# Turning gathered rows by DMA transposes of 16-bit halves, with y kept as planes of halves

## Chip, core and metric

The kernel runs on one core of one Trainium2 chip. The metric is the device time of one execution in microseconds (us). A core has five engines that work side by side, each through its own queue in order: TensorE (PE; its weight loads are shown as PEld), VectorE (DVE), ScalarE (ACT), GpSimd (POOL) and SyncE (SP), which here only issues DMAs. Sixteen DMA engines move data for the queues of SP and POOL.

## What is computed

First a filter along the sequence, through a real Fourier transform, for 8 sequences of 2496 rows with 256 channels. Then a mixture of experts on its 19,968 rows: each row goes to the two of 8 experts that score highest.

```python
y = irfft(rfft(x, axis=1) * (filt_r + 1j * filt_i), n=2496, axis=1)
x = y.reshape(19968, 256)
noisy = x @ w_gate + log1p(exp(x @ w_noise)) * noise
top2 = argpartition(-noisy, 2, axis=1)[:, :2]      # weights: softmax over the two
for e in range(8):
    for k in range(2):
        mask = top2[:, k] == e
        h = maximum(x[mask] @ w1[e], 0)            # w1: 256 x 1024
        out[mask] += top2_w[mask, k, None] * (h @ w2[e])   # w2: 1024 x 256
```

All of it is fp32. Products are made by splitting an operand into a rounded high part and the rest (`_split`, the pairs named h and l) and adding three matmuls (`_mm3`).

## The kernel before

**Stages.** `fft_stream` makes the filtered rows, one sequence ("batch", `bt`) after another, in halves of 128 channels (`n = 2 * bt + h`). The last step of a half, `i2` (L505), copies 117 x 512 values from PSUM into `yt` (L523) and stores them to `y` in DRAM (L527). A row of `y` has 256 channels and 8 gate weights, `YW` = 264 words. `gate` and `route` score the rows and write, for each expert, lists of row numbers (`lst`). The expert stage starts when the first batch is routed and runs beside the stream for the later batches; at the end it is alone.

**Blocks.** `expert` (L1068) works through blocks of 512 listed rows (`nt` = 4 tiles of 128) of one expert; two blocks in a row share an expert's weights from the third batch on (`PAIRS`). What is left is done in blocks of 256 (`UNIT`, `nt` = 2). For each block:

- `gather` (L986): POOL fetches rows of `y` by indirect DMA, 128 to a tile, into slots `xg` of the SBUF tile `stage` (L992). There are 8 slots, two blocks.
- `turn` (L999): the rows lie with rows on partitions, and the matmuls need channels on partitions. TensorE transposes each tile, for the channel halves `kc` = 0 and 1, into the PSUM bank `xps` (L1008); ACT rounds the high part into `mxh` (L1012) and DVE subtracts for `mxl` (L1013). POOL copies the expert's gate weights into `gt` (L1017).
- First layer (L1086 to L1100): for each of 8 slices f of the hidden width, six matmuls into a PSUM bank (`hps`, or for f = 2 and 5 one of the two `yps` banks, L1088), then ACT makes `hh` (L1095) and DVE `hl` (L1096).
- Second layer (L1109 to L1135): for each tile t, 16 or 24 matmuls into `yps` (L1120, L1121 or `_mm3`), scaled by the gate weight on ACT (L1125) and DVE (L1127) into a slot `yo`, and added to `out` by an indirect DMA of POOL (L1128).

`front` (L967) begins a block with new weights: `load_w` has SP load w1 and w2 through four slots `wst` (L1029), and `wsplit` splits them on ACT and DVE (L1057, L1058).

**What sets the order.** The kernel is written as Python generators, and a scheduler then orders the instructions of each engine by a timeline of its own, with data dependencies and buffer reuse kept. `pin` keeps some instructions in written order: those of the stream's opening, and POOL's gathers. In `expert` the next block's gather is written at the head of a block (`fetch`, L1061, at most two blocks ahead), and its `turn` between the two layers of the block before (L1104 to L1106). So the next block's rows are turned while the second layer runs. Each of `mxh0`, `mxl0`, `mxh1`, `mxl1` has one buffer, which the first layer of the block before must have read. Once built, every queue is in order: an instruction that waits holds all behind it on its engine, and SP's and POOL's DMA issues are such instructions.

## Time and profile before

| | us |
|---|---|
| three timed runs | 2311.85, 2312.91, 2316.61 (median 2312.91) |
| profiled execution, first to last instruction | 2318.9 |
| POOL: gathers (L992), busy | 328.8 (320 of 1.027) |
| POOL: scatters (L1128), busy | 526.9 (320 of 1.647) |
| ACT: `mxh` (L1012), busy | 96.8 (178 of 0.544) |
| DVE: `mxl` (L1013), busy | 113.1 (178 of 0.635) |
| HBM read, written | 221.98 MB, 105.78 MB |

The profile is of one execution and gives no other time for it than its span. Busy time of an engine is the time in which any of its instructions ran; matmuls are pipelined, so the start of one falls before the end of the one ahead, and the distance from start to start is what one costs the stream. The `idle before` of a group is the time its engine stood still just ahead of it, with what ended that. The profile's chain that ended last holds only the final scatter, so it says nothing on the middle of the run; slices and stretches do.

### The profile page before, as it was taken

The page shows a single profiled execution, that of the slowest core. Times are in us where ns is not written, and L with a number is a line of the kernel's source. Part 1 is how long each engine was busy: PE and PEld are TensorE (multiplying, and loading weights), DVE is VectorE, ACT ScalarE, POOL GpSimd, SP SyncE. Part 2 cuts the span into 40 slices and gives each one's busy share as a digit, 9 for nine tenths or more (in the row PEclk, how much of TensorE's full clock was granted, in tenths as well). Part 3 has the DMA queues.
Part 4 walks back from the last instruction along what each step waited for, and adds up shares of the span by engine and source line. Part 5 has one row for each costly group of instructions (what it writes and reads, how often), then busy time and mean ns, then how long its engine had stood idle before and what let it go on. Part 6 is the DMA issues. An engine that isn't in the chain of part 4 may idle for free. (4 is left out here: it accounts for less than half of the span.)

```text
span 2318.9 us, 39299 instructions
## 1 busy us (share of the span) xinstructions
PE 2263.9 (98%) x13089; PEld 1899.9 (82%) x13089; DVE 1544.4 (67%) x3331; ACT 1189.3 (51%) x2373; POOL 927.8 (40%) x827
## 2 busy tenths in 40 slices
PE   8889999999999999999999999999999999999998
PEld 6448888888788888888888888888888888889997
DVE  4866797778668665875669666954444445557886
ACT  6655646654554554444544444444444444446775
POOL 4014244332334334443434433544544454535442
PEclk9989999999999999999999999999999999999999
DMA  8677757665654555464454553444444445567773
GB/s 238 201 240 181 199 136 199 180 157 121 168 138 117 147 136 128 115 149 115 111 131 96 129 141 84 95 94 98 92 91 88 97 92 129 122 183 226 217 217 87
DMA packets 284723, 329.64 MB, mean 142 GB/s; under 512 B 37371, under 2 KB 197603, under 8 KB 284515
## 3 DMA queue, kind: packets, MB, share of 16 engines
q1 hardware_dynamic: 222435, 241.61, 34.4%
q0 software_dynamic: 62080, 85.47, 21.7%
q8 instruction: 105, 1.72, 0.3%
q14 instruction: 103, 0.84, 0.1%
HBM read 221.98 MB, written 105.78 MB: 141 GB/s over the span
## 5 line engine op out<-in xcount | busy, mean ns | idle before, releaser
L1120 PE MATMUL yps<-w,hh 128*128 128x512 f32 x2112 | 747.1, 398 | 0.0
L1128 POOL DMA_INDIRECT out<-stage,ids x320 | 526.9, 1647 | 330.5 <-DVE stage L1127 131.6
L1121 PE MATMUL yps<-w,hl 128*128 128x256 f32 x2112 | 570.9, 280 | 0.6 <-DVE hl L1096 0.6
L992 POOL DMA_INDIRECT stage<-y,ids x320 | 328.8, 1027 | 581.8 <-PE xps L1008 198.7
L121 PE MATMUL hps<-mxl,w1h 128*128 128x512 f32 (+1 forms) x1424 | 535.1, 376 | 0.0
L120 PE MATMUL hps<-mxh,w1h 128*128 128x512 f32 (+1 forms) x1424 | 526.5, 380 | 3.5 <-DVE hl L1096 1.5
L122 PE MATMUL hps<-mxh,w1l 128*128 128x512 f32 (+1 forms) x1424 | 527.1, 371 | 0.0
L1096 DVE SCALAR_TENSOR_TENSOR hl<-hps,hh 128x512 fp32r<-128x512 f32 (+1 forms) x712 | 438.5, 631 | 122.2 <-ACT hh L1095 117.7
L1095 ACT ACTIVATE hh<-hps 128x512 fp32r<-128x512 f32 (+1 forms) x712 | 381.2, 555 | 223.8 <-PE hps L122 204.3
L1120 PEld LDWEIGHTS yps<-w,hh 128*128 128x128 f32 x2112 | 389.2, 188 | 80.4 <-ACT hh L1095 0.3
L1121 PEld LDWEIGHTS yps<-w,hl 128*128 128x128 f32 x2112 | 396.9, 188 | 19.6 <-DVE hl L1096 1.0
L120 PEld LDWEIGHTS hps<-mxh,w1h 128*128 128x128 f32 x1424 | 265.7, 189 | 51.8 <-issue 4.1
L122 PEld LDWEIGHTS hps<-mxh,w1l 128*128 128x128 f32 x1424 | 269.0, 189 | 45.8
L121 PEld LDWEIGHTS hps<-mxl,w1h 128*128 128x128 f32 x1424 | 269.1, 189 | 40.6 <-issue 0.2
L1125 ACT ACTIVATE stage<-yps,gt 128x256 f32<-128x256 f32 x320 | 143.3, 474 | 284.6 <-PE yps L1121 140.0
L1127 DVE SCALAR_TENSOR_TENSOR stage<-yps,gt,stage 128x256 f32<-128x256 f32 x264 | 120.9, 479 | 196.5 <-ACT stage L1125 133.0
L1013 DVE TENSOR_TENSOR mxl<-xps,mxh 128x512 fp32r<-128x512 f32 (+1 forms) x178 | 113.1, 635 | 152.4 <-ACT mxh L1012 148.7
L1012 ACT CAST mxh<-xps 128x512 fp32r<-128x512 f32 (+1 forms) x178 | 96.8, 544 | 221.5 <-PE xps L1008 188.8
L1058 DVE TENSOR_TENSOR w<-stage,w 128x512 fp32r<-128x512 f32 x216 | 143.6, 685 | 29.3 <-ACT w L1057 23.9
L964 POOL CAST ids<-lt 128x8 int32<-128x8 f32 (+2 forms) x63 | 14.6, 231 | 369.4 <-DMA lt<-lst 330.4
L1058 DVE TENSOR_TENSOR w1l<-stage,w1h 128x512 fp32r<-128x512 f32 x180 | 123.7, 687 | 55.7 <-ACT w1h L1057 37.6
L1057 ACT CAST w1h<-stage 128x512 fp32r<-128x512 f32 x180 | 111.8, 621 | 95.5 <-PE hps L121 47.8
(222 smaller groups left out, 3073.8 us busy)
## 6 DMA issues: line engine op xcount, KB each, us to landing
stage<-w SPq DMA_DIRECT2D x396, 256.0 KB
x<-x SPq DMA_DIRECT2D x88, 256.0 KB
fd<-c SPq DMA_DIRECT2D x77, 240.0 KB
wb<-w SPq DMA_DIRECT2D x18, 1024.0 KB
fx<-fd SPq DMA_DIRECT2D x140, 128.0 KB
out<-z SPq DMA_DIRECT2D x24, 702.0 KB
y<-yt SPq DMA_DIRECT2D x40, 248.6 KB
y<-yt SPq DMA_DIRECT2D x40, 234.0 KB
```

The lines of the kernel that those rows point to most:

```text
L120: nc.tensor.matmul(o, lh, rh, start=start, stop=False)
L121: nc.tensor.matmul(o, lh, rl, start=False, stop=False)
L122: nc.tensor.matmul(o, ll, rh, start=False, stop=stop)
L992: self.pin(lambda: self.nc.gpsimd.indirect_dma_start(out=x, out_offset=None, in_=self.y[:BLK + ready * ROWS], in_offset=bass.IndirectOffse ...
L1058: nc.vector.tensor_sub(l, sv, f32v(h))
L1095: nc.scalar.activation(h, p, AF.Relu)
L1096: nc.vector.scalar_tensor_tensor(l, p, 0.0, f32v(h), op0=ALU.max, op1=ALU.subtract)
L1120: nc.tensor.matmul(bank, h, hl, start=(f == 0), stop=False)
L1121: nc.tensor.matmul(p, l, hl[:, 0], start=False, stop=(f == 7))
L1125: nc.scalar.activation(o, p, AF.Copy, scale=gate[:, t])
L1127: nc.vector.scalar_tensor_tensor(o, bank[:, 1], gate[:, t], o, op0=ALU.mult, op1=ALU.add)
L1128: a = nc.gpsimd.indirect_dma_start(out=self.io["out"][:BLK + ready * ROWS], out_offset=bass.IndirectOffsetOnAxis(ap=ids[:, t:t + 1], axis= ...
```

## The change

`y` now keeps each 128-channel half of a row as two planes of 16-bit halves: `i2` writes from PSUM, read as 16-bit, first the 128 low halves and then the 128 high halves. The bytes of a row are as many as before, and the gate weights stay as they were. The tensors are declared as 32-bit integers for the DMAs, which only carry them.

TensorE's transposes go. A new function `flip` has SP issue one DMA transpose of 16-bit elements for each gathered tile, 128 rows x 512 halves, into `xt`, [128, 4, 512] 16-bit with one buffer: channel on the partition, and for each `kc` a plane of low and a plane of high halves. POOL's copy of the gate weights moves into `flip`, and the register with the expert's number is loaded in `gather`. `turn` then has DVE put the halves together, a 16-bit copy from two planes into interleaved pairs in a slot `x32` of `stage` (one slot, used for both `kc`), and ACT and DVE split from there as before. `flip` is called after a gather is issued and at the end of each `turn`, and does nothing while a turned block has not been used.

To make room, `xg` has 4 slots instead of 8, `yo` 5 instead of 6, `stage` is 5120 words wide, and two tiles of the gate (`uh`, `oh0`) share buffers with `ut0` and `gl`. In the first layer f = 2 and f = 5 take the freed `xps` bank instead of `yps`.

```diff
-        self.y = self.dp.tile([NROW, YW], F32, name="y")
+        self.y = self.dp.tile([NROW, YW], I32, name="y")
...
-        at, n, w = {"wst": (0, 4, 512), "xg": (2048, 8, YW), "yo": (2048 + 8 * YW, 6, 256)}[nm]
+        at, n, w = {"wst": (0, 4, 512), "xg": (2048, 4, YW), "yo": (2048 + 4 * YW, 5, 256), "x32": (2048 + 4 * YW + 5 * 256, 1, 512)}[nm]
...
-            self.uh = P.tile([120, 24, 16], R32, name="uh")
+            self.uh = P.tile([120, 24, 16], R32, name="uh", tag="ut0", bufs=1)
...
-        nc.scalar.copy(yt[:, :k, :128], p[:RP, :m].rearrange("p (g d) -> p g d", g=k))
+        nc.scalar.copy(yt.bitcast(U16)[:, :k, :256].rearrange("p g (two d) -> p g two d", two=2),
+                       p.bitcast(U16)[:RP, :2 * m].rearrange("p (g d two) -> p g two d", g=k, two=2))
...
+    def flip(self):
+        e = next((e for e in self.ahead if not e[3]), None)
+        if e is None or self.turned is not None:
+            return
+        e[3] = True
+        nc, nt = self.nc, e[0][2]
+        xg, at, ra = e[2]
+        xt = self.P.tile([128, 4, 512], U16, name="xt", bufs=1)[:, :, :128 * nt]
+        for t in range(nt):
+            nc.sync.dma_start_transpose(xt[:, :, 128 * t:128 * t + 128], xg[t].bitcast(U16)[:, :2 * D])
+        gate = self.P.tile([128, 4, 1], F32, name="gt", bufs=3)[:, :nt]
...
+        nc.gpsimd.tensor_copy(gate, rows[:, :, bass.ds(ra, 1)])
+        self.turned = xt, gate
...
-            q = self.PS.tile([128, 512], F32, name="xps", bufs=1)
-            for t in range(nt):
-                nc.tensor.transpose(q[:, t * 128:(t + 1) * 128], xg[t][:, kc * 128:(kc + 1) * 128], self.ident)
+            q = self.slot("x32")
+            nc.vector.tensor_copy(q.bitcast(U16)[:, :2 * w].rearrange("p (t two) -> p two t", two=2), xt[:, 2 * kc:2 * kc + 2])
...
+        self.turned = None
         xT.append(gate)
+        self.flip()
         return xT
...
-                self.ahead.append((*p, self.gather(*p)))
+                self.ahead.append([*p, self.gather(*p), False])
+                self.flip()
...
-                p = self.PS.tile([128, 512], F32, name="hps", tag="hps" if f % 3 < 2 else "yps", bufs=2)[:, :w]
+                p = self.PS.tile([128, 512], F32, name="hps", tag="hps" if f % 3 < 2 else "xps", bufs=2 if f % 3 < 2 else 1)[:, :w]
```

What the scheduler makes of it shows at three places late in the run, where blocks of 512 rows come in pairs. On TensorE, before, where one block's second layer (`yps`) ends and the next one's first layer (`hps`) begins; the numbers in names tell tiles apart:

```order
L1121 MATMUL yps_20729<-w2_20452,hl_20633 128x256
L120 MATMUL hps_20806<-mxh0_20694,w1h_20669 128x512
L1008 MATMUL xps_20698<-ident_70,stage_83 128x128 x4
L121 MATMUL hps_20806<-mxl0_20695,w1h_20669 128x512
L122 MATMUL hps_20806<-mxh0_20694,w1l_20670 128x512
L1120 MATMUL yps_20709<-w2_20452,hh_20643 128x512
```

The same place now, where L1140 and L1141 are the old L1120 and L1121, and L121 to L123 the old L120 to L122:

```order
L1141 MATMUL yps_19892<-w2_19852,hl_19838 128x256
L121 MATMUL hps_19956<-mxh0_19856,w1h_19612 128x512
L121 MATMUL hps_19978<-mxh0_19856,w1h_19616 128x512
L1140 MATMUL yps_19872<-w2_19852,hh_19848 128x512
L1140 MATMUL yps_19892<-w2_19852,hh_19848 128x512
L122 MATMUL hps_19956<-mxl0_19857,w1h_19612 128x512
```

The four transposes are gone from between the first layer's matmuls, which still begin after two of the four second-layer groups. On SP, before, between the loads of w2 (L1029) and the register loads for the next list (`tabi`):

```order
L1029 ISA
L1029 DMA stage_83<-w2 128x512
L958 ISA
L958 DMA lt_17112<-lst_61 128x2x4
L973 TENSOR_LOAD tabi_15579
L973 ISA x2
L956 TENSOR_LOAD tabi_15579
```

And now (L1048 is the old L1029, L963 the old L958):

```order
L1048 ISA
L1048 DMA stage_83<-w2 128x512
L963 ISA
L963 DMA lt_16984<-lst_61 128x2x4
L1014 DMA_TRANSPOSE xt_16852<-stage_83 128x4x128 x4
L978 TENSOR_LOAD tabi_15478
L978 ISA x2
L961 TENSOR_LOAD tabi_15478
```

A block's four transposes stand in SP's queue behind the loads of w2 and the list. On DVE, before, from the split of a turned block (`mxl`) over the second layer's evictions (`yps`) to the next first layer's (`hl`):

```order
L1013 TENSOR_TENSOR mxl1_19104<-xps_19098,mxh1_19103 128x512
L1127 SCALAR_TENSOR_TENSOR stage_83<-yps_19109,gt_18903,stage_83 128x256
L1127 SCALAR_TENSOR_TENSOR stage_83<-yps_19129,gt_18903,stage_83 128x256
L1058 TENSOR_TENSOR w1l_19304<-stage_83,w1h_19303 128x512
L1127 SCALAR_TENSOR_TENSOR stage_83<-yps_19149,gt_18903,stage_83 128x256
L1096 SCALAR_TENSOR_TENSOR hl_19201<-hps_19193,hh_19200 128x512
```

And now (L1028 is the new copy, L1033, L1077, L1116 and L1147 the old L1013, L1058, L1096 and L1127):

```order
L1028 COPY stage_83<-xt_19184 128x2x512
L1033 TENSOR_TENSOR mxl1_19417<-stage_83,mxh1_19416 128x512
L1147 SCALAR_TENSOR_TENSOR stage_83<-yps_19427,gt_18967,stage_83 128x256
L1147 SCALAR_TENSOR_TENSOR stage_83<-yps_19447,gt_18967,stage_83 128x256
L1077 TENSOR_TENSOR w1l_19613<-stage_83,w1h_19612 128x512
L1028 COPY stage_83<-xt_19420 128x2x512
L1147 SCALAR_TENSOR_TENSOR stage_83<-yps_19467,gt_18967,stage_83 128x256
L1116 SCALAR_TENSOR_TENSOR hl_19519<-hps_19511,hh_19518 128x512
```

The copy that empties `xt_19184` lets SP transpose the following block into `xt_19420`, and only five rows later stands the copy that needs it, ahead of the third `yps` eviction and of the next block's `hl`.

More of the change, by code (lines that the diff above doesn't have):

```diff
@@ L965, in read_list, with front @@
         return ids, n, nt, s, self.tabs[i]
-    def front(self, blk, xg, fill=None):
+    def front(self, blk, fill=None):
         nc = self.nc
@@ L979, in front @@
             fill()
-        if fill and self.held_any:
-            xT = self.pin(self.turn, xg, nt, hold=False, only=[self.nc.tensor.engine])
-        else:
-            xT = self.turn(xg, nt)
+        xT = self.turn(nt)
         return w1, xT, w2st
@@ L996, in gather, with turn @@
             xg.append(x)
-        return xg, self.turns["xg"] + 1 - nt
-    def turn(self, xg, nt):
+        return xg, self.turns["xg"] + 1 - nt, self.ra
+    def flip(self):
[9 more added lines that the diff above has]
+        gate = self.P.tile([128, 4, 1], F32, name="gt", bufs=3)[:, :nt]
+        rows = self.stage[:, 2048:2048 + 4 * YW].rearrange("p (s w) -> p s w", w=YW)[:, at:at + nt, D:]
+        nc.gpsimd.tensor_copy(gate, rows[:, :, bass.ds(ra, 1)])
+        self.turned = xt, gate
+    def turn(self, nt):
         nc, P = self.nc, self.P
         xT = []
-        xg, at = xg
+        xt, gate = self.turned
         w = 128 * nt
         for kc in range(2):
-            q = self.PS.tile([128, 512], F32, name="xps", bufs=1)
-            for t in range(nt):
-                nc.tensor.transpose(q[:, t * 128:(t + 1) * 128], xg[t][:, kc * 128:(kc + 1) * 128], self.ident)
+            q = self.slot("x32")
+            nc.vector.tensor_copy(q.bitcast(U16)[:, :2 * w].rearrange("p (t two) -> p two t", two=2), xt[:, 2 * kc:2 * kc + 2])
             h = P.tile([128, 512], R32, name=f"mxh{kc}", bufs=1)
@@ L1014, in turn @@
             xT.append((h, l))
-        gate = P.tile([128, 4, 1], F32, name="gt", bufs=3)[:, :nt]
-        rows = self.stage[:, 2048:2048 + 8 * YW].rearrange("p (s w) -> p s w", w=YW)[:, at:at + nt, D:]
-        nc.gpsimd.tensor_copy(gate, rows[:, :, bass.ds(self.ra, 1)])
+        self.turned = None
         xT.append(gate)
+        self.flip()
         return xT
@@ L1078, in expert @@
             if cur is None:
-                cur = self.front(blk, xg, fill)
+                cur = self.front(blk, fill)
             w1, xT, w2st = cur
@@ L1104, in expert @@
             if self.ahead:
-                b2, i2, x2 = self.ahead[0]
-                cur = (w1, self.turn(x2, nt), None) if i2 else self.front(b2, x2, fill if late else None)
+                b2, i2 = self.ahead[0][:2]
+                cur = (w1, self.turn(nt), None) if i2 else self.front(b2, fill if late else None)
             self.fetch(may)
```

19 lines of the change are left out of this document (11 added, 8 removed).

## The prediction

> **What bounds the kernel now.** I read the page first: its head, the busy times, the forty slices.
>
> ```profile
> span 2318.9 us, 39299 instructions
> PE 2263.9 (98%) x13089; PEld 1899.9 (82%) x13089; DVE 1544.4 (67%) x3331; ACT 1189.3 (51%) x2373; POOL 927.8 (40%) x827
> PE   8889999999999999999999999999999999999998
> PEclk9989999999999999999999999999999999999999
> DMA  8677757665654555464454553444444445567773
> ```
>
> TensorE is idle for 2318.9 - 2263.9 = 55 us in all, and from the fourth slice on it is never under nine tenths, at the full granted clock. So the kernel is bound by TensorE's own work, not by a wait. Three stretches of 58 us (busy time of PE, PEld, DVE, ACT, POOL in turn; then clock, DMA share, GB/s) say how far the next engine is behind: a stretch with routing, one with experts alone, one with 256-row blocks.
>
> ```profile
> 1218.00:1276.00 58.00, 58.00 (x326) 48.33 (x325) 53.91 (x146) 26.51 (x52) 25.36 (x21) 1.00 0.44 98
> 1740.00:1798.00 58.00, 58.00 (x304) 49.01 (x303) 27.61 (x46) 24.62 (x47) 29.07 (x27) 1.00 0.42 90
> 2146.00:2204.00 58.00, 58.00 (x411) 54.01 (x410) 47.91 (x98) 41.47 (x98) 26.41 (x29) 1.00 0.74 219
> ```
>
> VectorE has 30 us to spare where experts run alone, but only 4 us where rows are routed and 10 us in the 256-row blocks.
>
> **What goes from TensorE.** The groups by line and shape give the transposes, and the stream of instructions shows what they hold up (start, duration; x4 is four in a row):
>
> ```profile
> L1008 PE MATMUL xps<-ident,stage 128*128 128x128 f32 x640 | 102.9, 274 | 12.3 <-DMA stage<-y,ids 5.4 <-issue 4.1 <-DVE mxl L1013 1.4
> 1502.58 0.60 PE L1008 MATMUL xps<-ident,stage 128*128 128x128 f32 x4
> 1502.93 0.47 PE L121 MATMUL hps<-mxl,w1h 128*128 128x512 f32 x1
> 1503.25 0.40 PE L122 MATMUL hps<-mxh,w1l 128*128 128x512 f32 x1
> 1503.48 0.40 PE L517 MATMUL q<-th,hl 120*117 120x512 f32 x1
> 2150.65 0.39 PE L1120 MATMUL yps<-w,hh 128*128 128x512 f32 x1
> 2150.88 0.27 PE L1121 MATMUL yps<-w,hl 128*128 128x256 f32 x1
> 2151.00 0.63 PE L1120 MATMUL yps<-w,hh 128*128 128x512 f32 x2
> ...
> 2151.82 0.38 PE L1008 MATMUL xps<-ident,stage 128*128 128x128 f32 x2
> 2151.95 0.36 PE L121 MATMUL hps<-mxl,w1h 128*128 128x256 f32 x1
> 2152.15 0.29 PE L122 MATMUL hps<-mxh,w1l 128*128 128x256 f32 x1
> 2152.28 0.62 PE L1120 MATMUL yps<-w,hh 128*128 128x512 f32 x2
> ```
>
> Busy times of pipelined matmuls overlap, so I don't take the 102.9 us; I take start to start. Four transposes hold the stream for 1502.93 - 1502.58 = 0.35 us, and the matmul behind them takes 0.32 us to the next start where its neighbour takes 0.23: 0.09 more. Together 0.44 us. Two transposes: 0.13 us, and 0.20 against 0.13 behind them: 0.20 us. A turn has two groups (kc = 0 and 1). Each turn makes two evictions on ACT and two on DVE, whose rows (quoted below) count 142 of 512 columns and 36 of 256, so 71 blocks of 512 rows and 18 of 256, 89 turns. Saved: 142 x 0.44 + 36 x 0.20 = 62.5 + 7.2 = **70 us**. Bounds: 142 x 0.35 + 36 x 0.13 = 54 us if the matmul behind keeps its delay, 102.9 us if the row's busy time were all exclusive.
>
> **What VectorE and ScalarE get.** DVE puts the halves together, 178 copies (142 of 1024 16-bit elements, 36 of 512), a kind that the trace lacks. The nearest rows:
>
> ```profile
> L1013 DVE TENSOR_TENSOR mxl<-xps,mxh 128x512 fp32r<-128x512 f32 x142 | 97.8, 689 | 143.7 <-ACT mxh L1012 141.8 <-issue 1.2
> L1013 DVE TENSOR_TENSOR mxl<-xps,mxh 128x256 fp32r<-128x256 f32 x36 | 15.3, 424 | 8.6 <-ACT mxh L1012 6.8
> L734 DVE TENSOR_SCALAR gz<-rank 117x176 f32<-117x176 f32 x8 | 2.0, 252 | 0.3
> L771 DVE TENSOR_TENSOR rank<-rank 117x176 f32<-117x176 f32 x40 | 13.6, 339 | 0.5
> L523 ACT COPY yt<-q 117x512 f32<-117x512 f32 x80 | 46.9, 586 | 35.2 <-PE q L517 21.4 <-PE q L516 5.1 <-PE q L513 4.7
> L523 ACT COPY yt<-q 117x256 f32<-117x256 f32 x16 | 6.1, 379 | 1.4 <-DMA y<-yt 0.6 <-ACT stage L1125 0.5 <-PE q L513 0.2
> L1095 ACT ACTIVATE hh<-hps 128x512 fp32r<-128x512 f32 x568 | 329.5, 598 | 204.1 <-PE hps L122 184.6 <-PE yps L122 4.9 <-issue 4.6
> L1096 DVE SCALAR_TENSOR_TENSOR hl<-hps,hh 128x512 fp32r<-128x512 f32 x568 | 381.5, 685 | 110.3 <-ACT hh L1095 105.8 <-issue 1.9 <-PE yps L122 0.7
> ```
>
> Two-source work costs (689 - 424) / 256 = 1.035 ns an element; at that rate a copy of 1024 takes 689 + 512 x 1.035 = 1.22 us. But a one-source operation in SBUF is cheaper: 252 against 339 ns at 176 elements, 87 ns less, half of 176 x 1.035. The copy is one-source in SBUF, so I take half rate: 0.69 us (0.42 for the small one). Added: 142 x 0.69 + 36 x 0.42 = 113 us (1.22 and 0.69: 198 us); DVE goes from 67% to some 74%. In the routing stretch about 2.2 turns bring 2.2 x 2 x 0.69 = 3.0 us into 4.1 us of room, and 5.4 us at the high price: 0 to 1.3 us over, in eight such stretches 0 to 10 us. The 256-row stretch takes 4.5 x 2 x 0.42 = 3.8 us into 10. I take 3 us. ACT's `yt` copy now names 1024 elements where it named 512: (586 - 379) / 256 = 0.81 ns each, so 80 x 0.41 + 16 x 0.21 = 36 us, hidden on an engine that is 51% busy; without that cover it would cost those 36 us. The banks: f = 2 and f = 5 now share one `xps` bank instead of two `yps` banks. Two groups of six matmuls at 0.23 us, 2.8 us, stand between them, and the eviction that must be through takes 0.60 on ACT and 0.69 on DVE, 1.28 us; so nothing, and if that cover is gone, the excess of a late eviction once in a block. In return the second layer no longer shares its `yps` banks. The turn's chain (copy, ACT, DVE, twice, through one `x32` buffer) is 2 x (0.69 + 0.60 + 0.69) = 4.0 us, 0.7 longer than with two groups of transposes. Beside it lie the two second-layer groups that TensorE's order puts before the next block's first matmuls, 16 pairs at 2151.00 - 2150.65 = 0.35 us, 5.6 us. Five `yo` slots for six and the gate's shared buffers I cost at nothing: TensorE, idle for 55 us in all, is not waiting for them today. If that cover is gone too, they belong to the late rows below.
>
> **What the DMA engines and SP get.** 320 transposes of 128 x 512 halves, 128 KB each. The trace has none; the nearest are the queues and SP's issues:
>
> ```profile
> q1 hardware_dynamic: 222435, 241.61, 34.4%
> q0 software_dynamic: 62080, 85.47, 21.7%
> L1029 SPq DMA_DIRECT2D stage<-w x360: 3/333/1957, 120.7 to 2062.0; - x180
> SPq L1029 <- DVE w1l L1058: 405.1, 119, 15.1
> L1128 POOL DMA_INDIRECT out<-stage,ids x320 | 526.9, 1647 | 330.5 <-DVE stage L1127 131.6 <-ACT stage L1125 111.5 <-issue 54.6
> ```
>
> SP's queue moves 241.61 MB in 34.4% of the span, 798 us: 0.43 us for 128 KB. POOL's moves rows of a kilobyte at 85.47 MB in 503 us: 0.77 us. Over 320 transposes that is 138 to 246 us on top of 34.4 + 21.7 = 56.1%, 1301 us: 62 to 67%, room enough. At the far end a transpose may go packet by packet, a 256-byte row of 128 halves each: 512 packets at POOL's 503 x 16 / 62080 = 0.130 us on one of 16 engines make 4.2 us, 320 of them 1331 us. I take 0.43 us, nearest in queue. An issue on SP costs between 0.33 us (median of L1029) and the 1.65 us that POOL spends on an indirect one; four per block are 1.3 to 6.6 us of some 26 us, so SP keeps up. But SP is in order and stands up to 15.1 us before a weight load that waits for a DVE split: transposes written behind such a load wait with it.
>
> For the DMA transpose the Trainium skill has two rules that disagree. VectorE: DVE Perf Modes, "The three transpose paths", lists 390 ns for a 128x128 of 16-bit on TensorE and 1309 ns through the DMA crossbar, and its rules say to use TensorE where PSUM will do: against this change. Advanced Engine Details and Errata, "X-Bar Transpose (TRN2)", calls them as fast as ordinary DMAs, 350 to 400 GB/s: by that 0.33 to 0.37 us for ours, the sum unchanged. This trace's TensorE transposes take 274 ns each but hold the stream for 0.09, so the first rule's comparison is not what is paid here; no run so far shows the crossbar.
>
> **Waits that are added.** Each turn's rows now pass gather, transpose, copy before ACT and DVE split them. In steady state a gather stands a whole turn ahead. The transposes can go when the turn before has emptied `xt`, and in DVE's order the copy that needs them comes five rows later, behind two evictions that wait for the 5.6 us of matmuls above. Issued one after the other they need 4 x 0.43 us and a landing of 3.1 us (below), 4.8 us: hidden, with little to spare. At 1.65 us an issue they need 9.7 us, and DVE stands for 4; but TensorE then still has the other two groups (5.6 us) and three first-layer slices (3 x 1.4 us) before it lacks a bank. Not covered is a start, where TensorE already waits for rows:
>
> ```profile
> 125.33 0.95 POOL L992 DMA_INDIRECT stage<-y,ids  x1 [0.30 <-issue]
> 129.38 0.48 PE L1008 MATMUL xps<-ident,stage 128*128 128x128 f32 x1 [1.90 <-DMA stage<-y,ids]
> 195.27 0.33 PE L1008 MATMUL xps<-ident,stage 128*128 128x128 f32 x1 [1.11 <-DMA stage<-y,ids]
> 595.51 0.33 PE L1008 MATMUL xps<-ident,stage 128*128 128x128 f32 x1 [2.41 <-DMA stage<-y,ids]
> ```
>
> A gather lands about 4.05 us after its start (129.38 - 125.33), 0.95 of it POOL's own. A transpose is a second landing, 3.1 us, with a copy of 0.69 us in place of 0.35: 3.4 us, and with its issue near 4 us; at three places 12 us (bounds 0, if other matmuls fill in, and 30 with the last transpose behind stores on SP). In the full stretches DVE's stand at that copy holds back the `yps` and `hl` evictions behind it, and TensorE stops when those banks are full. I take a mean of 0.1 us a turn, 9 us, near the end of 0 because TensorE has 9.8 us of its own work left when DVE stands for 4; the other end is the rival below. POOL's next gather also waits for the transposes, now with four slots, ahead of scatters; POOL waits hundreds of microseconds today without TensorE noticing, so nothing.
>
> Sum against this execution: 2318.9 - 70 + 3 + 12 + 9 = **2273 us**, a gain of 46. The profile gives only its span; the timed runs have a median of 2312.91, six less, so 2312.9 - 46 = **2267 us**.
>
> **Rivals.** (1) *Late transposes eat the gain.* Place: the DVE copy in front of evictions. For it: SP's 15 us stands, the DMA share of 0.74 in the 256-row blocks. Against it: 30 us of DVE room where experts run alone. Price: 89 x s for a stall s per turn, against 55 us of gain before it (70 - 15). Up to s = 0.62 us there is a gain; at s = 2 us it is 89 x 2 - 55 = 123 us slower, 2436. This is my rival on the slow side; a smaller s near 0.6 gives no change, 2313. (2) *The DMA engines become the bound.* Point: (2260 - 1301) / 320 = 3.0 us a transpose. At the far price of 4.2 us: 1301 + 1331 = 2632 us. By the Trainium skill's 1309 ns (VectorE: DVE Perf Modes, the section above), four squares in a row are 5.2 us and the time 1301 + 1676 = 2977 us, an estimate that counts its fixed part four times. Against it: q1's own rate. (3) *More is won:* all waits hidden and the matmul behind gains more, 2312.9 - 80 = 2233 or less. That the change doesn't do what it says is out: its program holds no L1008 matmul and 320 transposes on SP.
>
> **Numbers.** Forecast, gain of 20 to 80 us (2233 to 2293): 0.60. Small stalls (2293 to 2317): 0.12, of which 0.05 within 0.2% (4.6 us, about what a measurement here can tell from no change). Rival 1 proper (2318 to 2440): 0.16. Rival 2: 0.08. Rival 3: 0.04. So faster 0.60 + 0.07 + 0.04 = 0.71, same 0.05, slower 0.24. The range 2235 to 2345 leaves out rival 2, the upper half of rival 1 and the low end, some 0.2; the forecast's own is 2233 to 2293.
>
> **What would show it.** Right: PE busy near 2190, no L1008, PE idle under 80 us, the new copy at 0.69 us, DMA share up by 6 points. A copy at 1.22 us says the half rate is wrong. Idle PE time before `hps` or `yps` matmuls, ended by DVE, with DVE's copy waiting for a DMA, is rival 1; DMA near 1.0 all along is rival 2. Wrong would also be a turn's chain longer than the 5.6 us beside it.

## The result, and the profile after

The changed kernel takes 2340.78 us (median of 4 runs, 2337.98 to 2348.06) against 2312.38 us (2309.22 to 2316.61) for the kernel before beside it: a ratio of 1.013, 95% interval 1.0115 to 1.0145. It is 28 us **slower**; the forecast was 2267, 46 us faster. The profiled execution spans 2346.3 us, 27.4 more than before. First its page: head, busy times, slices, queues.

```profile
span 2346.3 us, 38867 instructions
PE 2234.9 (95%) x12449; PEld 1845.9 (79%) x12449; DVE 1635.6 (70%) x3509; ACT 1225.4 (52%) x2373; POOL 968.3 (41%) x827
PE   8769998999699999999999999999999999999997
PEclk9979999999899999999999999999999999999999
DMA  8697877785675766566656675555565556789884
q1 hardware_dynamic: 396515, 283.59, 45.9%
q0 software_dynamic: 62080, 85.47, 21.7%
```

TensorE's busy time fell by 29 us, not by 70, and its idle time rose from 55 to 111 us. There are two new dents, in the third and the eleventh slice, both with a lower granted clock. To place the loss I cut both traces at the same work: at the first `hh` of block 0, 12, 14, 42 and 72. Windows of the kernel before, then of the changed one (busy PE, PEld, DVE, ACT, POOL; clock, DMA share, GB/s):

```profile
0.00:160.20 160.20, 129.66 (x690) 80.14 (x691) 103.00 (x354) 98.67 (x193) 34.10 (x40) 0.96 0.78 231
160.20:537.70 377.50, 372.31 (x2449) 326.53 (x2448) 294.25 (x625) 215.68 (x425) 139.58 (x120) 1.00 0.67 173
537.70:614.70 77.00, 71.76 (x466) 61.17 (x465) 51.26 (x107) 36.41 (x74) 30.30 (x27) 0.96 0.60 152
614.70:1406.00 791.30, 789.65 (x4359) 656.33 (x4358) 548.95 (x1158) 383.96 (x749) 313.88 (x267) 1.00 0.52 126
1406.00:2106.60 700.60, 699.74 (x3724) 589.51 (x3723) 384.91 (x758) 313.53 (x606) 319.88 (x283) 1.00 0.48 109
2106.60:2318.90 212.30, 200.81 (x1412) 186.26 (x1410) 162.08 (x332) 141.03 (x331) 90.02 (x90) 0.98 0.65 185
```

```profile
0.00:174.70 174.70, 133.27 (x687) 81.45 (x688) 105.84 (x357) 108.43 (x193) 34.48 (x40) 0.93 0.81 218
174.70:552.60 377.90, 362.09 (x2307) 315.14 (x2305) 288.10 (x578) 218.47 (x414) 140.71 (x119) 0.99 0.78 186
552.60:654.60 102.00, 82.03 (x495) 66.83 (x494) 73.44 (x183) 45.94 (x87) 28.04 (x24) 0.87 0.57 139
654.60:1443.20 788.60, 778.34 (x4151) 638.39 (x4151) 582.09 (x1211) 397.75 (x750) 330.15 (x269) 1.00 0.65 145
1443.20:2121.30 678.10, 675.90 (x3476) 564.84 (x3474) 419.92 (x817) 311.91 (x603) 335.73 (x284) 1.00 0.61 133
2121.30:2346.30 225.00, 203.25 (x1344) 179.26 (x1342) 166.24 (x364) 142.90 (x331) 99.13 (x92) 0.97 0.78 197
```

The gain is there, but only in blocks 42 to 71 (the last of them already has 256 rows), mostly experts alone: 700.6 to 678.1, 22.5 us. With the stream beside it little changes (2.7 us gained in blocks 14 to 41, 0.4 lost in blocks 0 to 11). Lost are 14.5 us before the first block (the **start**), 25 in the **transition** (blocks 12 and 13, where the experts run out of the first two batches' rows) and 12.7 in the 256-row blocks. In the transition TensorE's idle time grew from 5.2 to 20.0 us. There the last second-layer matmul of block 13 and the first first-layer matmul of block 14 stand 6 us apart before and 46 us after (`yps` and `hps`; two lines of each timeline), with no matmul of the experts between them:

```profile
599.88 0.28 PE L122 MATMUL yps<-w,hl 128*128 128x256 f32 x1
605.94 1.65 PE L120 MATMUL hps<-mxh,w1h 128*128 128x512 f32 x3 [0.61 <-issue]
601.24 0.28 PE L123 MATMUL yps<-w,hl 128*128 128x256 f32 x1
646.97 1.65 PE L121 MATMUL hps<-mxh,w1h 128*128 128x512 f32 x3 [3.41 <-ACT mxh L1032]
```

The groups of the new work (line, engine, operation, count; busy us and mean ns; idle before, and what ended it), and from the view of line 1014 the issue of the transposes on SP (shortest, median, longest ns; first and last start):

```profile
L1028 DVE COPY stage<-xt 128x1024 uint16<-128x1024 uint16 x142 | 110.1, 775 | 184.4 <-DMA xt<-stage 169.3 <-issue 14.8
L1028 DVE COPY stage<-xt 128x512 uint16<-128x512 uint16 x36 | 17.0, 472 | 32.8 <-DMA xt<-stage 32.2 <-SPq L1217 0.4
L526 ACT COPY yt<-q 117x1024 uint16<-117x1024 uint16 x80 | 81.1, 1014 | 40.4 <-PE q L518 27.8 <-DMA y<-yt 8.0 <-PE q L514 3.8
```

```profile
L1014 SPq DMA_TRANSPOSE xt<-stage x320: 1189/1232/3980, 127.4 to 2311.0; - x160
```

VectorE stands 169 + 32 = 201 us for transposed rows. Two pieces of the timeline show where transposes hurt (start, duration; idle before, and its releaser). The start:

```profile
131.38 3.49 SPq L1014 DMA_TRANSPOSE xt<-stage  x1
...
132.52 1.02 ACT L526 COPY yt<-q 117x1024 uint16<-117x1024 uint16 x1
...
138.00 0.67 SPq L531 DMA_DIRECT2D y<-yt  x1
138.77 3.83 SPq L1014 DMA_TRANSPOSE xt<-stage  x1
...
146.90 1.01 ACT L526 COPY yt<-q 117x1024 uint16<-117x1024 uint16 x1 [5.33 <-DMA y<-yt]
...
147.97 1.21 PE L514 MATMUL q<-tf,cm 120*117 120x256 f32 x2 [8.00 <-ACT yt L526]
```

ScalarE's copy of 132.52 is done at 133.54, but SP sends its store only at 138.00: ahead of it in the queue stand a transpose whose issue takes 3.49 us and five other transfers. `yt` has two buffers here, so the copy of 146.90 waits for that store to land: ScalarE stands 5.33 us, and TensorE 8.00 us for ScalarE. Apart from the transpose nothing of the experts is in that chain. How much of the 8.8 us from the store's issue to its landing is the transposes' doing isn't shown; in the kernel before, a store issued at 128.69 took 9.4. And the 256-row blocks:

```profile
2207.85 0.46 DVE L1028 COPY stage<-xt 128x512 uint16<-128x512 uint16 x1
...
2207.96 0.39 SPq L1063 DMA_DIRECT2D wb<-w  x1
2208.53 2.69 SPq L1014 DMA_TRANSPOSE xt<-stage  x2
...
2217.36 0.45 DVE L1028 COPY stage<-xt 128x512 uint16<-128x512 uint16 x1 [4.18 <-DMA xt<-stage]
...
2218.78 0.39 PE L121 MATMUL hps<-mxh,w1h 128*128 128x256 f32 x1 [2.29 <-DVE hl L1116]
```

The next block's transposes go out once the copy has emptied `xt`, just behind a load of 1 MB of weights; VectorE stands 4.18 us for them, with the `hl` behind it, and TensorE stops for 2.29.

### The profile page after: what moved, and what is told of

It reads as the page before. It is cut to its first block, busy times and chain, and to the rows that moved or that the text cites. A ratio compares the mean times of both kernels' runs of the same rounds, so it can differ in the third digit from the quotient of the medians.

```text
span 2346.3 us, 38867 instructions
## 1 busy us (share of the span) xinstructions
PE 2234.9 (95%) x12449; PEld 1845.9 (79%) x12449; DVE 1635.6 (70%) x3509; ACT 1225.4 (52%) x2373; POOL 968.3 (41%) x827
## 3 DMA queue, kind: packets, MB, share of 16 engines
q1 hardware_dynamic: 396515, 283.59, 45.9%
## 5 line engine op out<-in xcount | busy, mean ns | idle before, releaser
L1140 PE MATMUL yps<-w,hh 128*128 128x512 f32 x2112 | 743.7, 400 | 8.0 <-ACT hh L1115 4.1
L1148 POOL DMA_INDIRECT out<-stage,ids x320 | 539.9, 1687 | 292.5 <-DVE stage L1147 123.4
L995 POOL DMA_INDIRECT stage<-y,ids x320 | 351.2, 1097 | 551.0 <-DMA xt<-stage 451.4
L1141 PE MATMUL yps<-w,hl 128*128 128x256 f32 x2112 | 552.4, 281 | 0.7 <-DVE rf L831 0.5
L122 PE MATMUL hps<-mxl,w1h 128*128 128x512 f32 (+1 forms) x1424 | 531.0, 375 | 1.9 <-DVE mxl L1033 1.9
L123 PE MATMUL hps<-mxh,w1l 128*128 128x512 f32 (+1 forms) x1424 | 526.7, 372 | 0.0
L1116 DVE SCALAR_TENSOR_TENSOR hl<-hps,hh 128x512 fp32r<-128x512 f32 (+1 forms) x712 | 435.4, 630 | 127.3 <-ACT hh L1115 124.4
L121 PE MATMUL hps<-mxh,w1h 128*128 128x512 f32 (+1 forms) x1424 | 505.0, 380 | 14.8 <-DVE hl L1116 8.9
L1140 PEld LDWEIGHTS yps<-w,hh 128*128 128x128 f32 x2112 | 383.2, 189 | 88.3 <-ACT hh L1115 7.5
L1141 PEld LDWEIGHTS yps<-w,hl 128*128 128x128 f32 x2112 | 395.2, 189 | 31.9 <-DVE rf L831 1.0
L121 PEld LDWEIGHTS hps<-mxh,w1h 128*128 128x128 f32 x1424 | 261.9, 189 | 67.5 <-DVE hl L1116 23.9
L123 PEld LDWEIGHTS hps<-mxh,w1l 128*128 128x128 f32 x1424 | 269.5, 189 | 49.1 <-issue 0.2
L122 PEld LDWEIGHTS hps<-mxl,w1h 128*128 128x128 f32 x1424 | 269.8, 189 | 44.7 <-DVE mxl L1033 3.2
L1028 DVE COPY stage<-xt 128x1024 uint16<-128x1024 uint16 (+1 forms) x178 | 127.1, 714 | 217.2 <-DMA xt<-stage 201.6
L1147 DVE SCALAR_TENSOR_TENSOR stage<-yps,gt,stage 128x256 f32<-128x256 f32 x264 | 120.8, 478 | 90.4 <-ACT stage L1145 89.9
L1077 DVE TENSOR_TENSOR w1l<-stage,w1h 128x512 fp32r<-128x512 f32 x180 | 123.4, 687 | 66.5 <-ACT w1h L1076 65.9
L1077 DVE TENSOR_TENSOR w<-stage,w 128x512 fp32r<-128x512 f32 x216 | 144.1, 685 | 14.1 <-ACT w L1076 13.7
L1032 ACT CAST mxh<-stage 128x512 fp32r<-128x512 f32 (+1 forms) x178 | 103.0, 579 | 96.5 <-DVE stage L1028 61.9
## 6 DMA issues: line engine op xcount, KB each, us to landing
out<-z SPq DMA_DIRECT2D x24, 702.0 KB
```

The source lines that it names most:

```text
L121: nc.tensor.matmul(o, lh, rh, start=start, stop=False)
L122: nc.tensor.matmul(o, lh, rl, start=False, stop=False)
L123: nc.tensor.matmul(o, ll, rh, start=False, stop=stop)
L995: self.pin(lambda: self.nc.gpsimd.indirect_dma_start(out=x.bitcast(I32), out_offset=None, in_=self.y[:BLK + ready * ROWS], in_offset=bass. ...
L1028: nc.vector.tensor_copy(q.bitcast(U16)[:, :2 * w].rearrange("p (t two) -> p two t", two=2), xt[:, 2 * kc:2 * kc + 2])
L1077: nc.vector.tensor_sub(l, sv, f32v(h))
```

## The experiments

Three theories. **A**: the transposes' landing, or their load, eats the gain. **B**: the fewer slots, and the program's order that follows from them. **C**: ScalarE's copy of `y`, which names twice the elements. All ratios are to the kernel before, with the 95% interval. For the runs that place the loss, the stages in us, cut as above. Each is one profiled execution, and a stage can move for reasons that no run here isolates: `late_t2` below, whose edit begins at block 50, is 11.5 us ahead of the kernel before at block 42.

| kernel | start | blocks 0-11 | 12-13 | 14-41 | 42-71 | 256 rows |
|---|---|---|---|---|---|---|
| before | 160.2 | 377.5 | 77.0 | 791.3 | 700.6 | 212.3 |
| changed | 174.7 | 377.9 | 102.0 | 788.6 | 678.1 | 225.0 |
| yt16 | 169.3 | 377.7 | 83.9 | 790.2 | 701.4 | 212.3 |
| yt_half | 169.9 | 383.1 | 92.0 | 779.3 | 676.9 | 221.3 |
| no_t8 | 165.7 | 372.1 | 88.9 | 782.8 | 675.7 | 214.7 |
| units2 | 172.7 | 376.0 | 100.4 | 791.3 | 678.9 | 216.5 |
| load_t | 173.4 | 411.2 | 68.8 | 792.1 | 706.1 | 245.9 |

**Slots.** Four gather slots in the kernel before (`slots`), then the same with the gather moved behind the turn that still needs the slots (`slots1`).

```diff
-"xg": (2048, 8, YW), "yo": (2048 + 8 * YW, 6, 256)
+"xg": (2048, 4, YW), "yo": (2048 + 4 * YW, 5, 256)
 # slots1 also, at the head of a block:
-            self.fetch(may)
+            if not self.ahead:
+                self.fetch(may)
```

> The kernel before, with four slots for gathered rows instead of eight and five output slots instead of six, and nothing else of the change. Theory A (the DMA transposes land late and load the DMA engines, and that eats the gain): slots cost nothing, 2312 +- 5 us. Theory B (the loss sits where batch 2 begins, because with four slots the program's order there falls differently and the gathers stand behind the last stores of y): slower by 10 to 25 us, 2322 to 2337, all of it between block 12 and block 14, which take 77 us before and 102 us in the changed kernel.

> The kernel before with four gather slots and five output slots, and the rows of a later block gathered only once the turn before it has read its own (the first of a block's two fetches is made only where nothing is ahead); in the earlier run with four slots a turn had to wait for the gather of the block behind it, so that run doesn't price the slots. Theory B (fewer slots): 10 to 25 us slower than before. Theories A and C: within 5 us of before.

`slots`: 1.0225 (1.0208 to 1.0242), in which each turn reads rows that the next gather has overwritten, and so waits for it. `slots1`: 1.019 (1.0172 to 1.0209). But `slots1` loses next to nothing in the start (161.5 us) and nothing in the transition (71.7), and 23 us in blocks 42 to 71 (723.4), where the changed kernel gains. The shorter lead of its gathers shows: over the run TensorE stands 32.1 us in 33 waits for gathered rows before a transpose, against 5.4 in 3 before. In the changed kernel, I take it, `xt` gives that lead back; no run shows that. Theory B as I put it falls: with `slots1`, four slots don't make the transition late.

**The copy of y.** The kernel before with the doubled element count alone (`yt16`), and the changed kernel with the single count (`yt_half`).

```diff
-        nc.scalar.copy(yt[:, :k, :128], p[:RP, :m]...)
+        nc.scalar.copy(yt.bitcast(U16)[:, :k, :256], p.bitcast(U16)[:RP, :2 * m]...)
 # yt_half, in the changed kernel:
+        nc.scalar.activation(yt.bitcast(I32)[:, :k, :128], p[:RP, :m]..., AF.Relu, scale=1000.0)
```

> The kernel before, with ScalarE's copy of y out of PSUM written as 1024 16-bit elements in their old places in place of 512 words: the same bytes, the doubled count. Theory C (the dearer copy on ScalarE is what makes the start 14.5 us later, since TensorE's idle time before the inverse transform, ended by that copy, went from 5 to 18 us): slower by 8 to 15 us, all of it before the first block of experts. Theories A and B: hidden, 2312 +- 5 us. In all cases the copy's row should read about 1.01 us.

> The changed kernel with ScalarE's copy of y at 512 elements again (a ReLU, scaled, into 32-bit integers, so that y isn't the reference's and its two halves are not kept apart); transposes, copies and slots stay. Theory C: 12 to 20 us faster than the changed kernel, 2321 to 2329, won before the first block and between blocks 12 and 14. Theory A: within 5 us of the changed kernel.

`yt16`: 1.0082 (1.0062 to 1.0103), 19 us slower. The groups of its profile, the row to set beside the 586 ns of before:

```profile
L523 ACT COPY yt<-q 117x1024 uint16<-117x1024 uint16 x80 | 80.9, 1011 | 32.0 <-PE q L517 20.5 <-PE q L513 5.8 <-DMA y<-yt 4.6
```

The same bytes cost 0.42 us more each. In the profiled execution 9.1 us are lost in the start and 6.9 in the transition, where I had expected none; next to nothing elsewhere. `yt_half`: 1.0024 (1.0006 to 1.0043), 1.06 points or about 25 us better than the changed kernel (each ratio is known to 0.2 points): 5 in the start, 10 in the transition, 9 in blocks 14 to 41, 4 in the 256-row blocks, and 5 lost again in blocks 0 to 11. Theory C holds, with 19 to 25 us. In the start the waits bear it out: TensorE stands 10.0 us for this copy in `yt16` between 60 and 185 us, against 5.3 before. In the transition they don't: no wait of TensorE there is ended by the copy in `yt16`, and 2.4 us of its 20 idle us in the changed kernel. By what path the copy costs time there stays open.

**Without the transposes.** The first two runs kept four slots, so that the copy had to wait for the gather of the next block (VectorE stands 228 us for gathers in `no_t`).

```diff
-            nc.sync.dma_start_transpose(xt[...], xg[t]...)      # no_t, no_t8; kept, unread, in nowait_t
-            nc.vector.tensor_copy(q..., xt[:, 2 * kc:2 * kc + 2])
+            nc.vector.tensor_copy(q..., rows[:, at:at + nt, 256 * kc:256 * kc + 256]...)
 # no_t8 also: "xg": (2048, 8, YW)
```

> The changed kernel without its 320 DMA transposes: VectorE's copy reads the gathered rows themselves (what the experts then get isn't turned). Everything else of the change stays. Theory A: the whole gain comes back and the time is 2312 less 54 (the 62 to 70 us of TensorE work at its low bound) plus some 5: 2260 to 2270. Theory B: the gain beside the transposes comes (some 10 us in the 256-row blocks and 10 where rows are routed), but the 25 us between blocks 12 and 14 stay lost: 2300 to 2320.

> The changed kernel with its 320 DMA transposes issued as they are, but into a buffer that nobody reads; VectorE's copy takes the gathered rows themselves, so nothing waits for a transpose to land but the slots of the gathered rows. What it has over the run without transposes is their load on the DMA engines and on SP's queue; what the changed kernel has over it is the wait for their landing. Theory A with the wait as the cause: within 5 us of the run without transposes. Theory A with the load as the cause: within 5 us of the changed kernel, 2341. Theory B: both within 25 us of the changed kernel.

> The changed kernel without its 320 DMA transposes and their buffer; VectorE's copy reads the gathered rows, which lie in eight slots as before the change, so that no gather lands on rows still to be read (in the earlier runs without a transpose, with four slots, the copy had to wait for the gather of the next block). The experts get rows that aren't turned. Theory A (the transposes' landing and load): about 2341 less 28 less 54, some 2260 to 2275. Theory C (ScalarE's dearer copy of y costs 16 to 20 us wherever TensorE waits for the stream, the transposes the rest): about 2275 to 2295, with the first block of experts still 9 us and the stretch from block 12 to 14 still 7 us later than in the kernel before.

`no_t` 1.022 (1.0203 to 1.0237) and `nowait_t` 1.0314 (1.0297 to 1.0331) are slower than the changed kernel through that wait; they price nothing. Only their difference says something: 0.9 points, 22 us, for transposes that nobody reads. `no_t8`: 0.9939 (0.9922 to 0.9957), 14 us faster than before and 1.9 points, 44 us, faster than the changed kernel. So the transposes cost 44 us, set against eight slots and the lead that these give in their place. Both theories had expected a larger gain (2304.31 us measured). Start and transition stay 5.5 and 11.9 us longer than before, 17.4 together. That is near the 16 of `yt16`; that the copy of `y` is all of it is argued, not shown.

**The one buffer in the 256-row blocks.**

```diff
-        xt = self.P.tile([128, 4, 512], U16, name="xt", bufs=1)[:, :, :128 * nt]
+        h = self.half_xt = (self.half_xt + 1) % 2 if nt == 2 else 0
+        xt = self.xt[:, 1024 * h:1024 * h + 512 * nt].rearrange("p (j c) -> p j c", j=4)
 # flip(): up to two blocks of nt == 2 may be turned ahead
```

> The changed kernel with the transposes' buffer cut in two for the 256-row blocks, so that a block's transposes are issued a whole block earlier and needn't wait until VectorE has emptied the one buffer. If the 12.7 us lost behind block 72 come from that wait (VectorE stands 28 us for transposed rows there): 8 to 13 us faster than the changed kernel, 2328 to 2333. If they come from the load on the DMA engines (share 0.78 there): within 4 us of it.

`units2`: 1.0068 (1.0049 to 1.0087), about 14 us better than the changed kernel; 8.5 of 12.7 us come back in the 256-row blocks, with the DMA share even higher (0.81). So most of the loss there was the wait for the buffer, not the load. The waits in those blocks (us, times, longest), in the changed kernel:

```profile
DVE stage L1028 <- DMA xt<-stage: 28.1, 14, 4.3
PEld hps L121 <- DVE hl L1116: 16.6, 26, 2.8
```

and in `units2`, where no wait of VectorE for a transpose remains there:

```profile
PEld hps L121 <- DVE hl L1117: 8.5, 19, 0.5
```

**The load alone.** Unread transposes beside the whole kernel before: of the gathered rows (`load_t`), of a block of zeros that is always ready (`load_z`), and ordinary DMAs of 128 KB in their place, one (`load_p1`) or two (`load_p2`).

```diff
 # in gather() of the kernel before, for each tile t:
+            nc.sync.dma_start_transpose(xt[...], xg[t].bitcast(U16)[:, :2 * D])      # load_t
+            nc.sync.dma_start_transpose(xt[...], self.z.bitcast(U16)[:, :2 * D])     # load_z
+            nc.sync.dma_start(xt[:, t % 3], self.z.bitcast(U16)[:, :2 * D])          # load_p1; two: load_p2
```

> The kernel before, whole, and beside it the 320 DMA transposes of the gathered rows, issued by SP behind each gather into a buffer that nobody reads (with five output slots and the shared buffers of the change, to make room). It prices the transposes' load on the DMA engines and on SP's queue alone; the landing costs nothing here but a gather slot. Theory A with the load as the cause of what the transposes cost: 20 to 44 us slower than before (44 is what the changed kernel lost to the run without transposes). With the landing as the cause: within 8 us of before.

> The run with unread transposes beside the kernel before, but they read a block of zeros that is ready from the start instead of the gathered rows: the same 320 issues and bytes on SP's queue, and nothing for them to wait for. If their traffic is the cause: the same 60 to 85 us over the kernel before. If SP's stand for the gathers is the cause: within 10 us of before; the 320 x 1.23 us = 394 us of issuing alone would fit into SP's idle time.

> The run with unread transposes of a block of zeros, with an ordinary DMA of the same 128 KB in the place of each transpose. If time of the DMA engines decides, and an ordinary DMA takes 0.43 us of them as the prediction had it for the transposes: half of the 168 us or less, 10 to 84 us over the kernel before, and the share of the engines in q1 some 6 points above its 34.4%. This is the load that the prediction reckoned with; if it costs under 10 us here, the prediction would have been right had a transpose cost what it said.

> The same with two ordinary DMAs of 128 KB for each transpose, so that the bytes are doubled and the engines' time is about the transposes' 0.87 us. If that time is what costs: about the 168 us of the run with transposes, 120 to 200 us over the kernel before. If it is the transpose's small packets or its 1.26 us on SP: well under, 20 to 90 us.

`load_t`: 1.0327 (1.0291 to 1.0362). Its transposes cost 13 us in the start, 34 in blocks 0 to 11 and 34 in the 256-row blocks, but only 6 in blocks 14 to 71, where some 230 of the 320 run. In all it is 76 us slower, more than either expectation, and it doesn't price the load alone: written right behind its gather, each transpose holds SP until the rows land, 443 us in all, against 8 in the changed kernel. `load_z` 1.0783 (1.0767 to 1.08), `load_p1` 1.0569 (1.0552 to 1.0587), `load_p2` 1.0869 (1.0851 to 1.0887): with nothing to wait for, they crowd into the front of the run, and cost only while they last (from block 42 on all three are within some 2 us of before in each stage). `load_z` lies far outside both its expectations, `load_p2` inside its 120 to 200 us. The queue's row in the pages of `load_z`, `load_p1` and `load_p2` (packets, MB, share of the 16 engines):

```profile
q1 hardware_dynamic: 396515, 283.59, 43.4%
```

```profile
q1 hardware_dynamic: 268515, 283.57, 38.2%
```

```profile
q1 hardware_dynamic: 314595, 325.53, 42.3%
```

Their last transfer starts at 959, 709 and 1121 us; an issue on SP takes 1256, 507 and 508 ns in the median. At block 14 all three are equally late (126, 124 and 117 us), and in the end 168, 122 and 187 us by their spans. Above the 798 us of before, q1's time is 282 us in `load_z` (43.4% of 2487.1), 135 in `load_p1` and 262 in `load_p2`: 0.88 us of the 16 engines for a transpose, 0.42 for an ordinary DMA of the same bytes. Half the engine time cost 73% of the loss: my expectation for `load_p1` (84 us at most) fell. In the front of the run all three kinds of transfer on SP's queue cost, in proportion neither to engine time nor to issue time (320 x 1.256 = 402, 320 x 0.507 = 162 and 640 x 0.508 = 325 us). How much of a transpose's cost is engine time and how much its place in the queue stays open.

**Another queue, a shared copy.**

```diff
-            nc.sync.dma_start_transpose(                                    # actq, in the changed kernel
+            nc.scalar.dma_start_transpose(
-        nc.scalar.copy(yt.bitcast(U16)[:, :k, :256]..., both halves)         # split2, in units2
+        nc.scalar.copy(yt.bitcast(U16)[:, :k, 128:256], pp[:, :, 1])
+        nc.vector.tensor_copy(yt.bitcast(U16)[:, :k, :128], pp[:, :, 0])
```

> The changed kernel with its transposes issued by ScalarE's DMA queue instead of SP's. If SP's order is what makes the start and the transition late (stores of y and loads of weights stand behind transposes that take 1.2 to 4.0 us each to issue): 5 to 15 us faster than the changed kernel, won before block 14. If ScalarE, which is in order too and would stand for the gathers and then 320 x 1.23 us = 394 us for the issues, pays more: 20 to 100 us slower. If the load alone counts: within 5 us.

> The changed kernel with the divided transposes' buffer of the run before (two halves in the 256-row blocks), and with the copy of y shared: ScalarE copies the upper halves, 512 elements, VectorE the lower ones. Nothing is left out. If the gains of the two runs that showed them add up (14 us for the buffer, 16 of the 24 us for the copy, since VectorE pays some of it where rows are routed): 2305 to 2320, about the time of the kernel before. If VectorE is too tight beside the stream: no better than the divided buffer alone, 2327 or more.

`actq`: 1.0701 (1.0675 to 1.0727). That is 5.7 points, about 132 us, above the changed kernel, more than the 20 to 100 expected. ScalarE is in order too: its evictions of `yps` stand 190.5 us, in 38 waits, for transposes. `split2`: 1.0185 (1.0165 to 1.0205), 1.2 points worse than `units2`. The start takes 183.3 us and blocks 0 to 11 389.8. Between 60 and 190 us ScalarE now stands 15.7 us for VectorE's part of the copy and VectorE 9.2 us for ScalarE's; that VectorE is too full there isn't shown (busy 118 of the start's 183 us).

**Transposes only where they gain.** `late_t` and `late_t2` put them into the kernel before for some of its late blocks; `y` stays in words.

```diff
+FROM, UPTO = 46, 71                      # late_t2: 50, 70, and a buffer pl for each tile
+            nc.vector.tensor_copy(pl[:, t]..., x.bitcast(U16)[:, :2 * D].rearrange("p (k d two) -> p k two d", ...))
+            nc.sync.dma_start_transpose(xt[:, :, 128 * t:128 * t + 128], pl[:, t])
```

> The kernel before with DMA transposes only in blocks 46 to 70 of 512 rows, where no stream runs beside the experts: y stays in words, VectorE sorts the gathered words into planes of halves (4 more copies of 512 elements a block), the transposes' buffers are those that the stream no longer needs; all other blocks turn on TensorE. Theories A and C both: the loss is in the start, the transition and the 256-row blocks, the gain in these 25 blocks, 0.69 to 0.76 us each: 17 to 19 us faster than before, 2296 to 2302, if VectorE's extra 1.9 us a block hide in the 12 us that it idles. If they don't: 2305 to 2320.

> The kernel before with DMA transposes only in blocks 50 to 69, after the stream has ended and before the 256-row blocks; the planes of halves of each gathered tile have a buffer of their own, so that VectorE's four sorting copies don't stand for transposes. If the gain of 0.69 to 0.76 us a block is there and VectorE's stands were what ate it in the run before: 20 x 0.7 = 14 us faster less up to 5 us for the first block, 2301 to 2310 (ratio 0.994 to 0.998). If VectorE's extra work or the transposes' landing takes it whatever the buffers: the same as before or up to 10 us slower.

`late_t`: 1.0103 (1.0079 to 1.0126): 17 us lost by its first block, and 9 more behind it. `late_t2`: 1.0029 (1.002 to 1.0039). It loses 8 us in blocks 48 and 49, where its first transposes are made ready, and wins nothing from block 50 to 70 (kernel before, then `late_t2`):

```profile
1608.00:2071.30 463.30, 462.97 (x2399) 390.74 (x2399) 233.14 (x385) 203.36 (x387) 211.61 (x192) 1.00 0.47 107
1604.80:2069.60 464.80, 454.43 (x2254) 376.11 (x2254) 276.84 (x484) 200.98 (x386) 211.79 (x186) 1.00 0.58 124
```

TensorE is busy for 8.5 us less and idles 10 us instead. The waits of `late_t2` there say for what: VectorE's sorting copies stand for gathers, ahead of evictions.

```profile
DVE pl L1085 <- DMA stage<-y,ids: 52.6, 47, 2.3
PEld hps L122 <- DVE stage L1150: 12.5, 12, 2.6
```

No complete version that I ran beats the kernel before.

## Why the prediction was wrong

**What goes from TensorE: right, near its low bound.** Forecast 0.88 us a turn, bounds 0.70 and more. In blocks 42 to 71 the changed kernel gains 22.5 / 30 = 0.75 us a block, without transposes 24.9 / 30 = 0.83. That the busy time fell by only 29 us is partly the granted clock, 0.982 in place of 0.993 over the span: at the old clock 2234.9 us would be about 2210 (an estimate, 2234.9 x 0.982 / 0.993).

**ScalarE's copy: the step "36 us, hidden on an engine that is 51% busy" failed.** Its price was right (0.41 us a copy; 1014 - 586 ns measured). But 51% is the span's mean. In the start TensorE waits for this very copy, and `yt16` charges 19 us over the whole run, `yt_half` returns 25. The waits of the kernel before had shown the place, 60 to 185 us, and I hadn't looked there. Before, and in the changed kernel:

```profile
PE q L513 <- ACT yt L523: 5.3, 6, 1.7
PE q L514 <- ACT yt L526: 18.4, 10, 8.0
```

**The DMA engines: "62 to 67%, room enough" was mis-sized.** A transpose takes 0.87 us of the engines ((45.9% of 2346.3 - 34.4% of 2318.9) / 320), not the 0.43 of an ordinary DMA; `load_p1` shows that 0.43 was right for that. And the mean share, 0.68, says nothing of the start (0.81) and the 256-row blocks (0.78). Whether room on the engines is what ran short isn't shown: in the 256-row blocks `units2` won time back at a share of 0.81. The Trainium skill's Advanced Engine Details and Errata, "X-Bar Transpose (TRN2)", calls such transposes as fast as ordinary DMAs; the runs say half as fast in engine time. The Trainium skill's VectorE: DVE Perf Modes, "Rules for kernel authors", advises TensorE where PSUM will do; the time agrees. The Trainium skill's VectorE: DVE Perf Modes, "The three transpose paths", lists 1309 ns a square, by which four would take 5.2 us, an estimate. Here one DMA of four squares takes 0.87 us of the engines and 1.23 us of SP.

**Starts and late transposes: 12 + 9 us forecast, mis-sized.** Start and transition lost 39.5 us; `no_t8` still loses 17.4 there, so the transposes' own part is near 22. With what `yt_half` returns the parts nearly add up: 9.0 and 4.8 of 14.5 in the start, 13.1 and 10.0 of 25.0 in the transition. In the start's longest wait the chain that I had costed, gather to transpose to copy, was not the one that decided: it was a store of `y` behind a transpose's issue. The 256-row blocks lost 12.7, where the wait for the single `xt`, which I had called hidden by 5.6 us of second layer, stood VectorE 28.1 us; two halves return 8.5. That is rival 1 with its place, its copy in front of evictions, in 18 blocks of 89.

**VectorE's tight stretches:** the copy costs 0.775 us, 0.69 forecast. In blocks 14 to 41, 28 x 0.75 = 21 us should have come and 2.7 did. Without transposes it is 8.5, with the short copy of `y` 12.0. So 5.8 us go to the transposes and 9.3 to ScalarE's copy, if the two add up, and some 3 remain, what I had forecast for VectorE. That split is argued: in the kernel before, `yt16` pays nothing for the same copy in these blocks (790.2 against 791.3).

**Put at nothing.** The five output slots and the gate's shared buffers held up where a run can tell: `load_p1` has both, and once its transfers are over it takes 787.9, 702.0 and 211.8 us for the last three stages, the kernel before 791.3, 700.6 and 212.3. A slip of reading changes no sum: TensorE's last slice reads 8, so it does fall under nine tenths there.

**The sum.** Gain by the low bound, 54 us; the copy of `y` back, 19 to 25; the transposes 44; that leaves 13 to 19 us, VectorE's copies and the order, to reach +28. The range did hold the time, at its edge, only because it took in half of rival 1; the forecast's own, 2233 to 2293, didn't. The scheduler's order may be a part of the transition, a rival that stays open: in the changed program the last five inverse transforms of batch 2 stand behind all matmuls of block 13, while before they stood among those of blocks 12 and 13. `no_t8` and `units2` have four or five of the five behind block 13 as well and take 89 and 100 us there; no run isolates it.

## What to carry to other kernels

Cost an edit in the stage where its engine is needed, not against a share of the span: 51% of ScalarE and 62% of the DMA engines hid nothing in the start, which took 14.5 us longer. A transfer added to an in-order queue is paid by whatever stands behind it there, here a store that has nothing to do with the experts. Work taken from the bound engine paid here only in the 30 blocks of 89 where hardly anything else ran beside the experts.

## What the runs showed of the hardware

- A DMA transpose of 128 x 512 halves (128 KB) is about 544 packets ((396515 - 222435) / 320) of some 240 bytes, 0.87 us of the 16 engines, and 1.19 to 3.98 us of issue on SP; an ordinary DMA of the same bytes 0.42 us, and 0.46 to 2.91 us of issue.
- ScalarE's copy out of PSUM goes by elements, not bytes: 1011 to 1014 ns for 1024 halves, 590 ns for 512 halves, and 586 ns for 512 words, twice their bytes.
- Where TensorE idled more, its granted clock was lower too: in the transition 0.87 with 20.0 us idle of 102.0 (before: 0.96, 5.2 of 77.0), and in the first 960 us of `load_z`, up to block 20, 0.91 with 162 us idle, where the kernel before has 0.99 with 41 us idle up to block 21:

```profile
0.00:960.00 960.00, 798.31 (x4575) 641.47 (x4576) 583.46 (x1393) 439.88 (x864) 271.10 (x242) 0.91 0.86 187
0.00:820.00 820.00, 778.84 (x4744) 637.00 (x4745) 601.00 (x1420) 455.27 (x896) 280.02 (x251) 0.99 0.65 173
```
